# One ring for the first loads, dilated rows of 12 tokens, earlier casts, and spreads moved into their own batch's stage

## The chip, the cores and the metric

The kernel runs on one core of a Trainium2 chip. The time is the device time of one execution in microseconds (us); a smaller one is better. A run of one core has no second die to be compared with, so "fast" below only says that a run lay within 1.5% of the fastest of its kernel. The rule cuts through a scatter without a gap: a run of 356.14 us counts as fast and one of 356.18 as slow, both with a granted clock of 0.986 (the granted clock is the recorded share of TensorE's full clock).

## The reference

Eight batches of eight heads attend over 576 tokens of 64 numbers. The attention output, 4608 tokens of 512 numbers, goes through a two-layer network with a gated activation. Condensed:

```python
rel = pos[:, None] - pos[None, :]
mask_plain = (rel >= 0) & (rel < 32)                             # heads 0 to 3
mask_dil = (rel >= 0) & (rel < 32 * 4) & (rel % 4 == 0)          # heads 4 to 7, every 4th token
attn = softmax(where(mask, q @ k.T / 8, -1e9)) @ v               # (8, 8, 576, 64)
x = attn.transpose(0, 2, 1, 3).reshape(4608, 512)
h = x @ w_in                                                     # 512 x 2048
g = h * (1 / (1 + exp(-beta * h)))
out = g @ w_out                                                  # 2048 x 512
```

Inputs and output are float32; the kernel multiplies in bfloat16.

## The kernel before

The 4608 tokens are worked off in nine blocks of 512. A block is a row of "slots" of four matmuls, 512 columns wide, of about 0.86 us each: 16 h slots (first layer) and, part of them carried into the next block, 16 output slots (second layer). Between the slots lie the small steps of the attention of the next batch: K and Q transpose loaded tokens, S makes scores, V multiplies with v, X transposes the result into `xT`, where the first layer reads it. So TensorE always has something large to do, as long as no step makes it wait.

```python
STEPS = (
    "S20 S21 S22 S23 V20 S30 V21 S31 V22 S32 V23 S33 V30 X20 S00 V31 S01 X21 V32 "
    "S02 V33 S10 V00 X30 S11 V01 S12 X31 V10 X00 V11 X01 X10 X11"
).split()
THIRD = (
    "d0 d1 v3 S20 S21 k0 S22 k1 S23 q0 V20 q1 S30 q2 V21 q3 S31 V22 S32 V23 S33 V30 X20 S00 V31 "
    "S01 X21 V32 S02 V33 v2 S10 V00 X30 S11 V01 S12 X31 V10 X00 V11 X01 X10 X11"
).split()
# FIRST and SECOND (batches 0 and 1) cut
```

The first two batches are loaded as tokens and transposed by TensorE. The rest goes a longer way (a "ring" is the queue into which an engine puts its DMA transfers): GpSimd's ring casts q and k to bfloat16 in DRAM, SyncE's ring loads them transposed, and VectorE then "spreads" them, that is, copies them into tiles in which the other head's half is zero. These copies are the small steps d, k and q.

```python
def load_tok(b, n, x):                      # x = 1: dilated heads
    R, T = (72, 8) if x else (64, 9)        # 72 rows of 8 tokens
    src = {"q": q, "k": k}[n][b, 4 * x:4 * x + 4].rearrange("h (a T) d -> a h (T d)", T=T)
    for lo, hi in ((0, 64), (64, R)):
        if lo < hi:
            nc.gpsimd.dma_start(out=dst[lo:hi], in_=src[lo:hi])

def spread_q(b, n, eng):                    # four of these per batch; k and dilated: two each
    e, hf = n % 2, (n % 2) ^ (n // 2)
    copy_on(eng)(
        out=qq[b % 2][64 * hf:64 * hf + 64, :, :, e],
        in_=raw[b, "q"][64 * e:64 * e + 64].rearrange("p (h i u) -> p h i u", h=4, i=NI))

# extras(b): what is issued beside the steps of batch b, for batch b + 1
    for name, (fn, i) in zip(
            ("S00 S01 S02 V33 S10 S11 S12 V10" if b > 2 else
             "V33 S10 V00 X30 S11 V01 S12 X31").split(), SPREADS):
        at(name, fn, b + 1, i, V)           # all eight spreads, in the second half of the stage
    at("X00", cast_v, b + 1, 3, G)          # v casts on GpSimd, at the stage's end
    at("X01", cast_v, b + 1, 2, G)
```

The order in which the loads enter the rings:

```python
load_vd(0, SQ)                              # v: SyncE's ring
load_vp_1(0, SQ, 0, 1, WIN)
for n in "kq":
    load_tok(0, n, 1)                       # k, q: GpSimd's ring
# ... plain heads of k and q, rest of v, four quarters of w_in
# ... after the steps of batch 0:
for g in range(2): load_w_out(g)
# ... tokens and v of batch 1
for g in range(2, 4): load_w_out(g)
for n in range(4): load_vp(2, G, n * NI, NI)
for kind in "kq": cast_qk(2, kind)
```

The softmax here doesn't subtract the row's maximum and nothing guards it: scores larger than these inputs give would overflow.

## Time and profile before

| | before |
|---|---|
| median of the first three runs | 353.56 us (353.46 to 356.23) |
| span of the profiled run | 352.4 us |
| TensorE busy | 317.4 us, 90% |
| VectorE busy | 209.1 us, 59% |
| longest stage with attention | third batch, 43.5 us; a steady one takes 34.3 |

The table is to be read in this way: the 35 us in which TensorE does nothing are the most that can be won while its own work stays the same, and the last row tells where a large part of them lies. The prediction below shows the lines themselves. To compare kernels I cut each trace where the first h slot of a token block begins, and count the length of each block and the idle time of TensorE in it. In this kernel the first block ends at 67.2 us, the second (with the third batch) at 110.8, the third at 144.4; the next three take 34.3 each, the one after 33.5.

### The profile page before, as it was taken

The numbers are of one execution on the slowest core, as the hardware profiler recorded it, in microseconds if no ns is written. First come the engines' busy times: TensorE is split into PE (matmuls) and PEld (weight loads), VectorE is DVE, ScalarE is ACT, GpSimd is POOL, SyncE is SP. The second block draws the span as 40 slices with busy tenths as digits, with TensorE's granted clock in tenths as the row PEclk, the third lists the DMA queues.
The fourth block names the chain that finished last, engine by engine and source line by source line (L and its number), as shares of the span: only waits on it lengthen the run. The fifth ranks groups of instructions, "written<-read, shape, count | busy, mean of one in ns | idle before, by whom it ended". The sixth has DMA issues, their size and how long they took to land.

```text
span 352.4 us, 6237 instructions
## 1 busy us (share of the span) xinstructions
PE 317.4 (90%) x2357; PEld 169.2 (48%) x2357; DVE 209.1 (59%) x430; ACT 196.2 (56%) x371; POOL 136.8 (39%) x178
## 2 busy tenths in 40 slices
PE   0998989986868998899999999999999999999995
PEld 0774555533433554455545545554555544444442
DVE  4368764679893689357936793688456344334400
ACT  1566756654634675566556656665666555345511
POOL 8954549044472546334643463436433100000000
PEclk9999999999998999999999999999999999999999
DMA  8999999998957990899189919991111111011131
GB/s 165 196 204 201 215 212 159 158 219 131 171 95 156 176 172 30 164 201 166 29 162 159 196 50 178 201 151 33 30 32 32 31 30 59 32 31 32 30 81 67
DMA packets 62671, 42.61 MB, mean 121 GB/s; under 512 B 46145, under 2 KB 56657, under 8 KB 62257
## 3 DMA queue, kind: packets, MB, share of 16 engines
q1 hardware_dynamic: 54128, 24.81, 38.1%
q0 software_dynamic: 8512, 17.40, 27.6%
q8 instruction: 18, 0.29, 0.4%
q14 instruction: 13, 0.10, 0.1%
HBM read 39.32 MB, written 16.52 MB: 158 GB/s over the span
## 4 chain that ended last, share of the span: by engine, by line
PE 79%; DVE 13%; ACT 4%; DMA 2%; issue 1%; POOL 0%; DVEq 0%; ACTq 0%; POOLq 0%
PE h_ps L464 30%; PE o_ps L495 29%; PE h_ps L495 4%; PE at L414 3%; DVE qq L279 3%; PE at L464 3%; PE at L431 3%; DVE xs L421 3%; DVE g L472 2%; PE at L388 2%; DMA xT<-in_k_dram 2%; DVE kz L271 2%; PE at L369 2%; PE at L381 1%; ACT osb L500 1%
## 5 line engine op out<-in xcount | busy, mean ns | idle before, releaser
L472 DVE SCALAR_TENSOR_TENSOR g<-tnh,h_ps 128x512 bf16<-128x512 bf16 x132 | 90.2, 685 | 90.7 <-ACT tnh L469 90.0
L464 PE MATMUL h_ps<-xT,w_in_bf 128*128 128x512 bf16 x528 | 132.9, 379 | 5.0 <-DVE g L472 4.5
L495 PE MATMUL o_ps<-w_out_bf,g 128*128 128x512 bf16 x512 | 130.4, 382 | 3.3 <-ACT osb L500 3.2
L469 ACT ACTIVATE tnh<-h_ps,beta_half 128x512 bf16<-128x512 f32 x132 | 90.7, 687 | 61.8 <-PE h_ps L464 56.3
L464 PEld LDWEIGHTS <-w_in_bf 128*128 128x128 bf16 x576 | 52.9, 98 | 57.4 <-issue 7.1
L495 PEld LDWEIGHTS <-g 128*128 128x128 bf16 x576 | 52.5, 98 | 54.4 <-issue 5.8
L394 ACT ACTIVATE pt<-at 128x384 bf16<-128x384 f32 (+2 forms) x112 | 48.4, 440 | 18.6 <-PE at L388 7.2
L396 POOL TENSOR_TENSOR pt<-pt,mask_d 96x384 bf16<-96x384 bf16 (+1 forms) x48 | 35.6, 752 | 57.4 <-ACT pt L394 56.9
L421 DVE TENSOR_TENSOR xs<-at,rcp 96x256 bf16<-96x256 f32 (+2 forms) x96 | 44.5, 464 | 14.8 <-PE at L431 10.8
L396 POOL TENSOR_TENSOR pt<-pt,mask_PP 128x384 bf16<-128x384 bf16 x24 | 23.6, 985 | 36.4 <-ACT pt L394 36.3
L500 ACT ACTIVATE osb<-o_ps 128x512 f32<-128x512 f32 x32 | 19.1, 597 | 25.6 <-PE o_ps L495 25.5
L414 PEld LDWEIGHTS <-pt 128*128 128x128 bf16 (+2 forms) x448 | 25.7, 101 | 15.0 <-POOL pt L396 2.3
L431 PE MATMUL at<-ident_b,xs 96*128 96x96 bf16 (+1 forms) x224 | 19.4, 203 | 7.2 <-DVE xs L421 4.4
L279 DVE COPY qq<-qpT 64x1152 bf16<-64x1152 bf16 x24 | 21.9, 912 | 0.5
L388 PEld LDWEIGHTS <-kdT 128*96 128x96 bf16 (+1 forms) x128 | 15.4, 128 | 13.9 <-issue 4.0
L388 PE MATMUL at<-qzd,kdT 128*96 128x192 bf16 (+1 forms) x128 | 19.2, 238 | 3.0 <-ACT qzd L357 1.6
L431 PEld LDWEIGHTS <-xs 96*128 96x128 bf16 (+1 forms) x224 | 13.4, 98 | 17.9 <-DVE xs L421 10.0
L414 PE MATMUL at<-vd,pt 96*128 96x65 bf16 (+1 forms) x256 | 19.5, 200 | 0.2 <-POOL pt L396 0.2
L417 DVE RECIPROCAL rcp<-at 96x4 f32<-96x4 f32 (+2 forms) x96 | 16.7, 174 | 3.7 <-PE at L414 3.3
L396 POOL TENSOR_TENSOR pt<-pt,mask_FP 128x384 bf16<-128x384 bf16 x12 | 12.8, 1065 | 15.5 <-ACT pt L394 15.5
L441 ACT COPY xT<-at 128x288 bf16<-128x288 bf16 x24 | 9.4, 398 | 16.5 <-PE at L431 16.5
L495 PE MATMUL h_ps<-w_out_bf,g 128*128 128x512 bf16 x64 | 15.5, 379 | 0.0
(92 smaller groups left out, 232.5 us busy)
## 6 DMA issues: line engine op xcount, KB each, us to landing
vp_st<-in_v_dram SPq DMA_DIRECT2D x10, 384.0 KB, 8.7
qk<-in_k_dram POOLq DMA_DIRECT2D x6, 576.0 KB, 5.5
qk<-in_q_dram POOLq DMA_DIRECT2D x6, 576.0 KB, 8.3
vd_st<-in_v_dram SPq DMA_DIRECT2D x6, 384.0 KB, 5.4
w_in_bf<-in_moe_w_in_dram POOLq DMA_DIRECT2D x4, 512.0 KB, 9.1
w_out_bf<-in_moe_w_out_dram POOLq DMA_DIRECT2D x4, 512.0 KB, 12.8
out_dram<-osb SPq DMA_DIRECT2D x8, 256.0 KB, 3.6
vd_st<-in_v_dram SPq DMA_DIRECT2D x6, 320.0 KB, 6.3
```

The lines of the kernel that those rows point to most:

```text
L279: copy_on(eng)(out=qq[b % 2][64 * hf:64 * hf + 64, :, :, e], in_=raw[b, "q"][64 * e:64 * e + 64].rearrange("p (h i u) -> p h i u", h=4, i=NI))
L388: nc.tensor.matmul(sc[0:K, a, 0:2 * n], lhsT=kd[b][:, rp, h4, DO[hf]:DO[hf] + K], rhs=qzd[b % 2][:, :, rp, h4, hf * DQ[0]:hf * DQ[0] + n], ...
L394: nc.scalar.activation(out=w, in_=sc[0:K, :, 0:2 * n], func=ACT.Exp, scale=SCALE)
L396: nc.gpsimd.tensor_tensor(out=w, in0=w, in1=mask[0:K], op=ALU.mult)
L414: nc.tensor.matmul(pv[:, a, h2, :], lhsT=pt[x][0:K, c:c + P], rhs=rhs, start=True, stop=True)
L421: nc.vector.tensor_tensor(out=xs_t[b, x, jx][:, a0:a0 + m], in0=pv[0:n, :, :, 0:D], in1=rcp[0:n, 0:m].unsqueeze(3).to_broadcast([n, m, 2, ...
L431: nc.tensor.transpose(xp[:, a * n:(a + 1) * n], xs[:, a].rearrange("p h d -> p (h d)"), ident_b[0:n, 0:n])
L464: nc.tensor.matmul(hps, lhsT=w_in_bf[:, kt, fb * P:(fb + 1) * P], rhs=xT[:, kt, t * NTOK:(t + 1) * NTOK], start=(kt == 0), stop=(kt == NKT ...
L469: nc.scalar.activation(out=tnh[:], in_=hps, func=ACT.Tanh, scale=beta_half[:, fb:fb + 1])
L472: nc.vector.scalar_tensor_tensor(out=g[:], in0=tnh[:], scalar=1.0, in1=hps, op0=ALU.add, op1=ALU.mult)
L495: nc.tensor.matmul(ops[:], lhsT=g_t[t, fb][:, tb * P:(tb + 1) * P], rhs=w_out_bf[:, fb, :], start=(fb == 0), stop=(fb == NFB - 1))
L500: nc.scalar.mul(out=osb[:], in_=ops[:], mul=0.5)
```

## The change: its intent, and the diff

VectorE is to lose work where it holds TensorE up. The key and query spreads go from the previous batch's stage to their own batch's, the zero fills to GpSimd, and the third batch's v casts to ScalarE. The start is to come sooner: dilated k and q go first on GpSimd's ring, v behind them, each in one transfer of 48 rows of 12 tokens. And the third batch's casts go ahead of the second half of the output weights, so that its data is there when its stage begins. All of the third batch's v goes to SyncE's ring, and two half groups of h matmuls (H0, H1) go ahead of the first batch's last transposes.

```diff
 STEPS = (
-    "S20 S21 S22 S23 V20 S30 V21 S31 V22 S32 V23 S33 V30 X20 S00 V31 S01 X21 V32 "
+    "S20 S21 S22 k0 S23 k1 V20 S30 q0 V21 S31 q1 V22 S32 q2 V23 S33 q3 V30 X20 S00 V31 S01 X21 V32 "
...                                         (FIRST, SECOND, THIRD in the same way; H0, H1 in FIRST)
-    FROM = {1: 6}
+    FROM = {1: 2}
-        nc.vector.memset(kz[i][64:128, :, :, 0], 0.0)
-        nc.vector.memset(kz[i][0:64, :, :, 1], 0.0)
+            nc.gpsimd.memset(kz[i][64:128, :, :, 0], 0.0)
+            nc.gpsimd.memset(kz[i][0:64, :, :, 1], 0.0)
...                                         (smaller bias tiles, keys of the first batches moved into xT)
-        R, T = (72, 8) if x else (64, 9)
+        R, T = (48, 12) if x else (64, 9)
-        for lo, hi in ((0, 64), (64, R)):
-            if lo < hi:
-                nc.gpsimd.dma_start(out=dst[lo:hi], in_=src[lo:hi])
+        nc.gpsimd.dma_start(out=dst, in_=src)
...                                         (3 instead of 2 transposes per head and pair; crossed query copies)
-            eng = (nc.scalar if b == 1 and name == "v2" else
+            eng = (nc.scalar if name[0] == "v" and (b, name) in ((1, "v2"), (2, "v0"), (2, "v1"), (2, "v2")) else
...                                         (an h group can begin with two of its four matmuls: H0, H1)
-                for name, (fn, i) in zip(
-                        ("S00 S01 S02 V33 S10 S11 S12 V10" if b > 2 else
-                         "V33 S10 V00 X30 S11 V01 S12 X31").split(), SPREADS):
-                    at(name, fn, b + 1, i, V)
+                at("S11", spread_dil, b + 1, 0, V)
+                at("V01", spread_dil, b + 1, 1, V)
-    load_vd(0, SQ)
-    load_vp_1(0, SQ, 0, 1, WIN)
     SQ.dma_start(out=beta_row[:], in_=moe_beta.rearrange("(f p) -> f p", p=P))
     for n in "kq":
         load_tok(0, n, 1)
     make_identity(nc, ident_b[:])
+    load_vd(0, G)
...                                         (another deal of the steps to the slots of the first blocks; a v cast counts as one unit of work)
+    for kind in "kq":
+        cast_qk(2, kind)
     zeros(1)
+    for kind in "kq":
+        load_dil(2, kind)
+    for kind in "kq":
+        load_plain(2, kind)
     for g in range(2, 4):
         load_w_out(g)
-    for n in range(4):
-        load_vp(2, G, n * NI, NI)
-    for kind in "kq":
-        cast_qk(2, kind)
+    zeros_kz()
```

## The prediction

> **What bounds the kernel now.** I read four views. First the page, for the share of each engine; then busy time by stage; then the timeline of TensorE, adding up the idle time in brackets; then the chain of waits, to see what the idle time was spent on.
>
> The page, with its slices of 1/40 of the span (8.8 us each):
>
> ```profile
> PE 317.4 (90%) x2357; PEld 169.2 (48%) x2357; DVE 209.1 (59%) x430; ACT 196.2 (56%) x371; POOL 136.8 (39%) x178
> PE   0998989986868998899999999999999999999995
> DVE  4368764679893689357936793688456344334400
> PEclk9999999999998999999999999999999999999999
> DMA  8999999998957990899189919991111111011131
> ```
>
> TensorE is the bound, with 35 us in which it does nothing, and these 35 us are nearly all in the first 14 slices. Cut by stage (start of batch 0; its rest; the 16 h slots of the first token block; its output slots with the second batch; the block with the third batch; with the fourth; one in steady state):
>
> ```profile
> 0.00:8.70 8.70, 0.01 (x1) 0.04 (x2) 4.30 (x17) 1.49 (x2) 7.22 (x18) 1.00 0.87 165
> 8.70:28.90 20.20, 18.55 (x230) 15.20 (x231) 11.46 (x31) 12.42 (x27) 14.51 (x23) 1.00 1.17 200
> 28.90:43.20 14.30, 14.03 (x68) 6.32 (x69) 11.66 (x22) 10.68 (x16) 7.77 (x11) 1.00 1.15 211
> 43.20:67.20 24.00, 21.33 (x279) 13.91 (x278) 14.62 (x36) 15.05 (x33) 11.84 (x23) 1.00 1.07 181
> 67.20:110.70 43.50, 33.12 (x237) 16.86 (x236) 34.38 (x61) 20.89 (x42) 19.19 (x21) 0.97 0.91 156
> 110.70:144.50 33.80, 30.78 (x238) 16.30 (x237) 24.36 (x48) 20.47 (x41) 16.21 (x18) 0.99 0.71 131
> 178.90:213.20 34.30, 33.47 (x253) 17.76 (x252) 22.91 (x48) 21.53 (x42) 16.63 (x18) 1.00 0.87 145
> ```
>
> Columns: the stretch, its length, busy us of TensorE, weight loads, VectorE, ScalarE, GpSimd; granted clock, DMA share, GB/s. The losses are 8.7 us before the first transpose, 2.7 in 43 to 67, 10.4 in the third batch's stage (67.2 to 110.7), where VectorE is busy 34.4 of 43.5 us, 3.0 in the next, 0.83 in each later one. The last 71 us have no attention, and the change cannot touch them.
>
> Who delays TensorE in the third batch's stage (the chain of waits, in order of time):
>
> ```profile
> 78.51 1.22 DVE kz L271
> 79.75 0.81 DVE kz L271
> 83.38 0.70 DVE kz L139
> 84.27 0.70 DVE kz L140
> 95.63 1.42 DVE vp L310
> ...
> 100.03 1.05 DVE qq L279
> 101.10 1.08 DVE qq L279
> 103.02 1.22 DVE qq L279
> 104.25 1.62 DVE qq L279
> 107.76 3.20 PE o_ps L495 x8
> ```
>
> From 74 to 107 us the chain is almost one line of VectorE work. After the stall TensorE's eight matmuls take 3.20 us instead of 1.73: it restarts at a lower clock, which the eight and the four behind them pay with 1.7 us.
>
> **What the Trainium skill says.** "GPSIMD Engine Reference", section "8. Key points": GpSimd shares its SBUF interfaces with VectorE, with contention when VectorE is in a two-port mode or has two SBUF inputs. The trace agrees: the same query spread (64x1152 bf16) took 0.45 us when GpSimd was idle (81.2 us) and 1.05 to 1.6 us beside its masks and casts (100 to 106 us). "TensorE: Matmul & The Clock Gate", Part 1: an idle array falls back to half its clock. The trace shows it at 107.76 as above. "PSUM — Partial Sum Buffer", section "PSUM bank collisions raise a hardware error": engines on one bank must be kept apart. Here ScalarE's copy of a query tile waits for VectorE's copy of the other half (2.2 us over two waits for qzd, 3.6 over two for qq). "DMA: Bandwidth & Descriptors", section "Issuing engines are not separate DMA queues": all rings run on the same 16 engines and interleave. In the trace 704 KB of v, issued on SyncE at 0.82, landed at 5.1 and 6.6 us; k and q, issued on GpSimd from 1.34, at 8.6 and 9.5.
>
> **The change part by part.**
>
> Start. Dilated k and q now come first on GpSimd's ring, one transfer each instead of two, with v behind them; SyncE's ring has only beta. 288 KB at the 200 KB/us of this stretch take 1.4 us; with issue (1.34 to about 2.1), and about 2 us of start and landing, k should be there at about 5.5 and q at 6.8 instead of 8.55 and 9.5. Against it: rows of 12 tokens make three transposes per head and pair instead of two, 48 instead of 32; one took 2.08/32 = 65 ns, so +1.0 us here. K from 5.5 to 7.1, Q to 8.7. Then the query copies: the two tiles go in crossed order, so VectorE (0.71) and ScalarE (0.65) work on different banks; the tile of the first score block is ready after about 1.4 us, at 10.1, instead of 11.8. The smaller bias tiles (96 and 48 columns instead of 384 and 192) save GpSimd about 2.5 us of building, so the next loads are issued earlier. Gain **2.0 us** (estimate, 1.3 to 2.6). From there to 28.9 TensorE has no gap over 0.2 us until 27.6, so the shift carries through.
>
> End of batch 0. Half of two h groups (dilated heads) goes ahead of the last transposes: four matmuls, 0.86 us, into gaps of 0.46, 0.46 and 0.27. **-0.7**.
>
> First block, with the second batch. Its steps now start at the 11th slot, one per slot, and no longer all after the h slots. Gone are the waits for qzd (1.42 + 0.17) and for qq (0.74): the transposes have one to three slots of 0.86 us to be copied behind. Of 2.7 us I take off 2.2; 16 more transposes at 1.20/32 = 37 ns add 0.6. **-1.6**.
>
> Third batch's stage. Its casts go ahead of half the output weights, and 768 KB of its v leave GpSimd's ring for a later place on SyncE's. The casts landed at 57.0 and 60.9, the last transposing load at 71.7, and the stage's steps began at 75. Moved up, I estimate casts at 46 to 49 and the last load at about 60. VectorE loses here: the key and query spreads of the fourth batch, 0.55 + 0.56 + 2.14 + 2.86 = 6.1 us; two zero fills, 1.4 (the other two lie just before the stage; all go to GpSimd, early); the v casts, 1.22 + 1.42 = 2.6, now on ScalarE at about 3 us. That is 10.1 of 34.4. What is left, 24 us, must fit into TensorE's time. That floor: the steady stage has 32 slots of 0.865 = 27.7 us, 0.83 idle, so its attention costs 34.3 - 27.7 - 0.8 = 5.8; this stage has 28 slots, 24.2 + 5.8 = 30.0. ScalarE would have 24, VectorE 24 of it, so it is tight, and I give it 0.8 of the ordinary idle time and 2 of new stalls: 32.8 instead of 43.5, **-10.7**.
>
> Fourth batch's stage. TensorE's gaps of 0.74 and 1.34 behind VectorE's spreads go (they are now early in the stage), with about 0.3 of slow clock at its start. **-2.4**.
>
> Later stages. The same eight spreads per stage, moved from the second half to the first, where four divisions and GpSimd's masks also are. I add **+0.5** over five stages for new waits.
>
> Output weights. Their third quarter landed at 47.2 and was used at 57.9; behind 1152 KB of casts and beside the transposing loads I estimate it lands at 51 to 54 and is wanted at 53. **+0.4**.
>
> Sum: -2.0 - 0.7 - 1.6 - 10.7 - 2.4 + 0.5 + 0.4 = -16.5; 353.6 - 16.5 = **337 us**.
>
> **The rivals.**
> (1) ScalarE takes VectorE's place. It gets 3 us of casts into a stage that shrinks by 11, and a cast waiting for v would hold up every tanh behind it. For it: ScalarE serves tanh, exp and copies strictly in order, and v of the third batch is now issued behind four transposing loads. Against: 24 of 33 us, and 4 us of estimated slack for v. It would give back 3 to 5 us: 341.
> (2) The DMA rings set the time. The 16 engines are full until 53 us in both kernels, and the order alone changes. If the output weights come 3 us late or the transposing loads at 65, TensorE waits in 50 to 65: 341 to 343. Against: neither was waited for before, by 10 us for the weights.
> (3) The start does not move: the first load's time is latency and not sharing. Then 339.
> (4) The crowded first half of the later stages costs 1 us each: 341. For it: spreads are doubled in length by GpSimd; against, VectorE is busy only 23 of 34 us there.
> (5) The stage reaches its floor, and the start gains more: 333.
>
> **Range and chances.** The large term, VectorE's 10 us on the chain, is well supported; what can fail is what replaces it. One or two of the rivals together give 341 to 343, the good case 332. The 2% line is 346.5, so two thirds of the gain must fail to miss it. **Range 332 to 343**; faster by over 2% 0.93, within 2% 0.06, slower 0.01.
>
> **What would show it.** The first transpose at about 5.5 us (8.7 before) and the first bias matmul of scores with its keys at about 10; the first output slots' gaps behind qzd and qq gone; in the third batch's stage TensorE idle under 3.5 us, VectorE about 24 us busy, no slow matmuls at its end; its length near 33 us; the later stages near 34.3. It would be wrong if TensorE showed waits on ScalarE's tanh behind v casts, on output weights around 53 us, or on VectorE's g behind spreads in each later stage.

## The result, and the profile after

The changed kernel took 342.57 us (median of four runs, 341.58 to 343.61) where the kernel before took 354.76 on the same chip (four runs). The ratio is 0.9655, with a 95% interval from 0.9598 to 0.9713. Here and below a ratio is the mean time of one kernel's fast runs over that of the other's of the same rounds, so it is not quite the ratio of the quoted medians. The result is correct.

The page of the changed kernel; of the slices, each is 8.5 us long:

```profile
PE 311.3 (92%) x2347; PEld 168.0 (49%) x2389; DVE 194.0 (57%) x424; ACT 197.8 (58%) x374; POOL 129.7 (38%) x170
PE   1899996997899899999999999999999999999994
DVE  4578773469657774767386637763865344244400
DMA  6999999999899794979698968882001210011121
GB/s 109 211 207 208 166 233 176 198 217 205 141 141 189 128 197 102 172 182 129 131 142 183 127 125 160 176 124 63 18 14 33 62 33 32 32 31 33 41 82 62
```

VectorE is busy 15 us less, and TensorE's 86868 in the 9th to 13th slice (its line in the prediction) has become 97897. Two new things show. In the first slice the DMA engines move 109 GB/s, where it was 165. And TensorE has a 6 in its 7th slice, 51 to 59 us, where it had a 9.

What sets the end has changed hands. This is the head of the chain of waits on both pages, the kernel before first:

```profile
PE 79%; DVE 13%; ACT 4%; DMA 2%; issue 1%; POOL 0%; DVEq 0%; ACTq 0%; POOLq 0%
```

```profile
PE 72%; DMA 13%; DVE 4%; ACT 4%; POOL 3%; issue 2%; POOLq 0%; ACTq 0%
```

VectorE's 13% have become 4%, as intended; DMA's 2% have become 13%. A chain follows one path only, so 13% is no loss of 13%; but it says which kind of wait to look for.

By stage (until the first transpose; rest of batch 0; first token block; third batch's stage; the fourth's; one in steady state; columns as in the prediction; here and below some stretches begin or end 0.1 to 0.3 us before the first h slot):

```profile
0.00:6.50 6.50, 0.00 (x0) 0.00 (x0) 2.78 (x15) 1.49 (x2) 5.05 (x16) 1.00 0.58 89
6.50:24.90 18.40, 16.19 (x228) 13.56 (x229) 11.00 (x29) 10.48 (x24) 13.31 (x22) 1.00 1.17 205
24.90:66.40 41.50, 36.96 (x375) 21.34 (x380) 27.32 (x61) 26.35 (x52) 20.65 (x31) 1.00 1.18 198
66.40:101.50 35.10, 30.50 (x234) 16.16 (x238) 23.58 (x50) 24.04 (x46) 15.60 (x18) 1.00 0.96 176
101.50:133.20 31.70, 29.81 (x234) 16.10 (x237) 22.17 (x48) 20.55 (x41) 16.18 (x19) 1.00 0.86 155
166.80:200.40 33.60, 32.94 (x248) 17.76 (x252) 21.47 (x48) 21.44 (x42) 16.09 (x18) 1.00 0.89 151
```

VectorE's busy time in the third batch's stage (fourth line) fell from 34.4 to 23.6 us, and TensorE's idle time there from 10.4 to 4.6. The first block begins at about 25 partly because half an h group now goes ahead (without it, in a run below, it begins at 26.0, against 29.0 in the kernel before); it is its end that can be compared. The stages by the starts of their first h slots, with what each was predicted to give:

| stage | before | after | difference | predicted |
|---|---|---|---|---|
| end of the first block | 67.2 | 66.4 | -0.8 | -3.9 (start, half groups, first block, weights) |
| third batch's stage | 43.5 | 35.2 | -8.3 | -10.7 |
| fourth batch's stage | 33.7 | 31.7 | -2.0 | -2.4 |
| the next four | 34.3, 34.3, 34.3, 33.5 | 33.6 each | -2.0 | +0.5 |
| the last two, without attention | 28.5, 43.1 | 28.5, 43.5 | +0.4 | 0 |
| whole span | 352.4 | 339.9 | -12.5 | -16.5 |

(The parts are rounded.) Most of what is missing against the prediction lies ahead of 67 us. TensorE's timeline of the kernel before at its first work (start, length, what; in brackets the idle time before it and its releaser):

```profile
8.69 2.08 PE L328 MATMUL at<-ident_b,xT 72*128 72x72 bf16 x32 [8.69 <-DMA xT<-in_k_dram]
...
11.79 0.48 PE L388 MATMUL at<-qzd,kdT 128*96 128x192 bf16 x2 [0.69 <-DVE qzd L357]
```

The changed kernel, at its first work and at 54 us:

```profile
6.54 1.14 PE L327 MATMUL at<-ident_b,xT 48*128 48x48 bf16 x24 [6.54 <-POOL neg_d L162]
8.63 1.14 PE L327 MATMUL at<-ident_b,xT 48*128 48x48 bf16 x24 [0.96 <-DMA xT<-in_q_dram]
...
11.04 0.48 PE L391 MATMUL at<-qzd,kdT 128*96 128x192 bf16 x2 [0.78 <-ACT qzd L357]
...
53.93 0.33 PE L378 MATMUL at<-qq,xT 128*128 128x192 bf16 x2
57.38 1.02 PE L508 MATMUL h_ps<-w_out_bf,g 128*128 128x512 bf16 x4 [3.12 <-DMA w_out_bf<-in_moe_w_out_dram]
```

The first transpose starts 2.15 us sooner (the first bracket names GpSimd, but the keys landed at 6.49, so it is the load that counts). Then the new wait: q lands at 8.59, and TensorE stands for 0.96 us between the keys' transposes and the queries'. The first scores with keys gain only 0.75 us. And at 57.38 an output slot had waited 3.12 us for the third quarter of the output weights. It landed at 57.3; before it landed at 47.2.

A second thing differs in this stretch. The same pair of score matmuls at about the same time, in the kernel before and in the changed one:

```profile
22.49 0.53 PE L375 MATMUL at<-qq,kz 128*128 128x192 bf16 x2
```

```profile
22.19 0.33 PE L378 MATMUL at<-qq,xT 128*128 128x192 bf16 x2
```

In both traces these small matmuls are slow at first, one taking up to 0.37 us, and 0.24 us later. The trace's first record of the full clock stands at 25.9 us in the kernel before and at 21.9 in the changed one; the clock column of the stretches above shows 1.00 there all the same, because it counts only recorded lowered stretches. This time is not a fixed property of a kernel: in the traces of the experiments it lies anywhere from 14.6 to 27.9 us.

The third batch's stage is no longer a line of VectorE work. The chain of waits there (start, us, what) now reads:

```profile
75.70 1.03 ACT vd L312
...
78.07 1.03 DVE kz L270
...
80.36 0.76 DVE qq L278
...
82.91 0.47 DVE qq L278
...
84.81 0.46 DVE qq L278
85.27 0.47 DVE qq L278
85.78 0.33 PE at L384 x4
...
100.16 1.67 PE o_ps L508 x7
```

The query spreads are the third batch's own; the fourth's, which took 1.05 to 1.62 us each at the end of this stage before, are gone from it. So is the slow clock: seven matmuls at 100.16 take 1.67 us.

The later stages got shorter, which I had not expected. The end of one of them, kernel before, TensorE and then VectorE:

```profile
210.41 0.30 PE L431 MATMUL at<-ident_b,xs 96*128 96x96 bf16 x3
211.18 0.30 PE L431 MATMUL at<-ident_b,xs 96*128 96x96 bf16 x3 [0.46 <-ACT xT L441]
```

```profile
206.74 0.80 DVE L279 COPY qq<-qpT 64x1152 bf16<-64x1152 bf16 x1
208.29 1.31 DVE L279 COPY qq<-qpT 64x1152 bf16<-64x1152 bf16 x1
210.56 0.55 DVE L421 TENSOR_TENSOR xs<-at,rcp 96x384 bf16<-96x384 f32 x1
```

And in the changed kernel:

```profile
198.64 0.42 PE L434 MATMUL at<-ident_b,xs 96*128 96x96 bf16 x6
198.90 1.89 PE L508 MATMUL o_ps<-w_out_bf,g 128*128 128x512 bf16 x8
```

Before, the next batch's last spreads ran beside GpSimd's v casts just when the last normalisations (`xs`) were due. The last two groups of transposes came one after the other, with 0.46 us of idle time between them, and the stage ended on that. Now the six transposes go in one group. In the prediction I had looked at where the spreads were going and not at what they had held up where they were.

### The profile page after: what moved, and what is told of

It is laid out like the page before. It is cut to its first block, busy times and chain, and to the rows that moved or that the text cites. A ratio compares the mean times of both kernels' runs of the same rounds, so it can differ in the third digit from the quotient of the medians.

```text
span 339.9 us, 6236 instructions
## 1 busy us (share of the span) xinstructions
PE 311.3 (92%) x2347; PEld 168.0 (49%) x2389; DVE 194.0 (57%) x424; ACT 197.8 (58%) x374; POOL 129.7 (38%) x170
## 4 chain that ended last, share of the span: by engine, by line
PE 72%; DMA 13%; DVE 4%; ACT 4%; POOL 3%; issue 2%; POOLq 0%; ACTq 0%
PE o_ps L508 31%; PE h_ps L475 29%; DMA w_out_bf<-in_moe_w_out_dram 5%; DMA xT<-in_q_dram 5%; PE h_ps L508 3%; DMA vp_st<-in_v_dram 3%; PE at L417 3%; PE at L434 2%; PE at L384 2%; ACT osb L513 2%; DVE g L485 2%; PE at L391 2%; DVE qq L278 1%; ACT tnh L482 1%; POOL pt L399 1%
## 5 line engine op out<-in xcount | busy, mean ns | idle before, releaser
L485 DVE SCALAR_TENSOR_TENSOR g<-tnh,h_ps 128x512 bf16<-128x512 bf16 x130 | 88.7, 684 | 90.4 <-ACT tnh L482 89.6
L475 PE MATMUL h_ps<-xT,w_in_bf 128*128 128x512 bf16 x504 | 129.6, 379 | 3.3 <-DVE g L485 2.1
L508 PE MATMUL o_ps<-w_out_bf,g 128*128 128x512 bf16 x494 | 126.3, 379 | 4.7 <-ACT osb L513 3.8
L482 ACT ACTIVATE tnh<-h_ps,beta_half 128x512 bf16<-128x512 f32 x130 | 89.3, 687 | 56.3 <-PE h_ps L475 51.9
L475 PEld LDWEIGHTS <-w_in_bf 128*128 128x128 bf16 x576 | 51.7, 98 | 51.5 <-issue 3.5
L399 POOL TENSOR_TENSOR pt<-pt,mask_d 96x384 bf16<-96x384 bf16 (+1 forms) x48 | 36.9, 778 | 52.0 <-ACT pt L397 51.4
L399 POOL TENSOR_TENSOR pt<-pt,mask_PP 128x384 bf16<-128x384 bf16 x24 | 22.8, 949 | 37.8 <-ACT pt L397 37.7
L434 PE MATMUL at<-ident_b,xs 96*128 96x96 bf16 (+1 forms) x224 | 18.1, 200 | 1.1 <-DVE xs L424 1.0
L399 POOL TENSOR_TENSOR pt<-pt,mask_FP 128x384 bf16<-128x384 bf16 x12 | 10.9, 910 | 16.0 <-ACT pt L397 16.0
L448 ACT COPY xT<-at 128x384 bf16<-128x384 bf16 (+1 forms) x32 | 12.6, 394 | 3.5 <-PE at L434 3.5
```

Of the source, the lines that this page charges most:

```text
L399: nc.gpsimd.tensor_tensor(out=w, in0=w, in1=mask[0:K], op=ALU.mult)
L434: nc.tensor.transpose(xp[:, a * n:(a + 1) * n], xs[:, a].rearrange("p h d -> p (h d)"), ident_b[0:n, 0:n])
L475: nc.tensor.matmul(hps, lhsT=w_in_bf[:, kt, fb * P:(fb + 1) * P], rhs=xT[:, kt, t * NTOK:(t + 1) * NTOK], start=(kt == 2), stop=(kt == 1))
L482: nc.scalar.activation(out=tnh[:], in_=hps, func=ACT.Tanh, scale=beta_half[:, fb:fb + 1])
L485: nc.vector.scalar_tensor_tensor(out=g[:], in0=tnh[:], scalar=1.0, in1=hps, op0=ALU.add, op1=ALU.mult)
L508: nc.tensor.matmul(ops[:], lhsT=g_t[t, fb][:, tb * P:(tb + 1) * P], rhs=w_out_bf[:, fb, :], start=(fb == 0), stop=(fb == NFB - 1))
```

## The experiments

Each run is compared with runs of the kernel before on the same chip. The changed kernel itself ran beside them only in the last call; where a difference to the change is given in us for the earlier runs, it is one of medians from different calls, and the ratios to the kernel before show it smaller or not at all (their intervals often overlap with that of the change). In the call with four of the runs (the kernel before with the spreads moved, v casts on VectorE, rows of 8, no early half) three of the seven runs of the kernel before were slow; the record calls these four comparisons unclear at its 2% line. What carries the readings are the traces: the length of a stage that an edit does not touch repeats within 0.1 us from trace to trace. Theory A is that the change is worth what it takes off VectorE's chain, above all by the spreads, and that the rest of the expected gain was lost in the order and the speed of GpSimd's DMA ring. The rivals are named with each run.

### The casts behind the weights again

```diff
+    for g in range(2, 4):
+        load_w_out(g)
     for kind in "kq":
         cast_qk(2, kind)
...
-    for g in range(2, 4):
-        load_w_out(g)
```

> The changed kernel with one part undone: the second half of the output weights goes ahead of the third batch's casts again. The theory that the order on GpSimd's ring is what TensorE's 3.12 us wait at 57.4 us pays for: the third quarter of the weights lands about 4 to 5 us earlier (near 52) and that wait is gone, while the casts and the transposing loads land about 5 us later (last near 69) and the third batch's first steps wait for them: 1 to 4 us come back at about 68 us. Net 340 to 345 us. Rival, that the early casts are worth most of the third stage's gain: over 347 us, with VectorE and TensorE idle for over 4 us at the third batch's start. Rival, that the third stage has slack for late casts: 339 to 340, the wait simply gone.

Measured: 339.20 us (338.75 to 339.49), ratio to before 0.9612 [0.9560, 0.9664]. The first block and the third batch's stage of this kernel:

```profile
25.40:64.00 38.60, 37.31 (x381) 21.27 (x378) 27.83 (x61) 26.28 (x52) 18.64 (x27) 1.00 1.13 190
64.00:99.10 35.10, 30.76 (x239) 16.15 (x238) 23.58 (x50) 24.13 (x46) 17.02 (x21) 1.00 1.07 198
```

The expected 340 to 345 us was too high; the last rival, slack in the third stage, is what came. The first block is idle 1.3 us instead of 4.5, the wait for the weights is gone, and yet the third batch's stage takes the same time as in the change, though its casts landed at 56.5 and 59.2 instead of 51.3 and 54.1 and its last transposing load at 66.7 instead of 64.3. So the earlier casts gained nothing, and cost about 3 us (2.4 between the two traces, 3.4 between the medians). That last load had been at 71.7 in the kernel before, with casts at 57.0 and 60.9: with the transposing loads issued right behind the casts it lands 7.5 us after the last cast instead of 10.8. Whether the stage needs even that was not tried.

### v on SyncE's ring again

```diff
+    load_vd(0, SQ)
+    load_vp_1(0, SQ, 0, 1, WIN)
     SQ.dma_start(out=beta_row[:], ...)
...
-    load_vd(0, G)
...
-    load_vp_1(0, G, 0, 1, WIN)
```

> The changed kernel with the first v loads back on SyncE's ring at the start. Theory that one ring alone starts slowly and shifts all that stands behind it: the first transposes start later, at 8 us instead of 6.5, but the last input weights land about 1.5 to 2 us earlier (26.5 to 27 instead of 28.6) and the wait for the output weights shrinks from 3.1 to 1.3 to 2 us; total within 1 us of the changed kernel (341.5 to 343.5). Rival, that the ring makes no difference to the total of what the engines move: input weights land at the same time, the start's loss of 1.5 us stays in full, 343.5 to 344.5.

Measured: 341.33 us (340.56 to 342.90), ratio 0.9679 [0.9627, 0.9730]. The first stretch and the first block:

```profile
0.00:9.20 9.20, 0.01 (x1) 0.01 (x1) 2.78 (x15) 1.49 (x2) 7.45 (x22) 1.00 0.95 153
28.70:66.70 38.00, 37.02 (x382) 21.19 (x380) 27.25 (x61) 26.27 (x52) 18.94 (x29) 1.00 1.19 196
```

The first transpose starts at 9.19, 2.65 us later than in the changed kernel. But the DMA engines are busy from the start (153 GB/s over the first 9.2 us; 89 over the first 6.5 in the changed kernel), the last input weights land at 27.9 instead of 28.6, the first block has no wait for output weights (idle 0.98), and it ends at 66.7 instead of 66.4. The 2.65 us that the new order gains at the start are paid back at 54 us by the ring.

### The k and q spreads back in the previous batch's stage

```diff
-    "S20 S21 S22 k0 S23 k1 V20 S30 q0 V21 S31 q1 V22 S32 q2 V23 S33 q3 V30 ..."
+    "S20 S21 S22 S23 V20 S30 V21 S31 V22 S32 V23 S33 V30 ..."
...
+                for name, (fn, i) in zip(
+                        ("S02 V33 S10 V00 S12 V10" if b > 2 else
+                         "V00 X30 S11 V01 S12 X31").split(),
+                        [(spread_k, 0), (spread_k, 1)] + [(spread_q, n) for n in range(4)]):
+                    at(name, fn, b + 1, i, V)
```

> The changed kernel with the key and query spreads of the fourth and later batches back in the stage before their own, in its second half. Theory that they cost VectorE time on the chain at the end of each stage: the third batch's stage grows by 3 to 5 us, and each later stage by 0.5 to 0.7 (last transposes wait again, a gap near 0.46 us before the last one): 346 to 350 us. Rival, that the gain of the later stages came from somewhere else (the order of the h groups' halves, PSUM banks): later stages stay at 33.6 and only the third grows.

Measured: 357.64 us (357.33 to 358.17), ratio 1.0137 [1.0091, 1.0182], so 15 us slower than the change. That is beyond the expected 346 to 350. The third batch's stage, the fourth's and a later one:

```profile
68.10:108.30 40.20, 32.59 (x238) 16.52 (x238) 28.89 (x56) 24.18 (x46) 16.84 (x18) 0.96 0.92 169
108.30:144.40 36.10, 31.42 (x238) 16.41 (x237) 25.11 (x48) 20.47 (x41) 16.32 (x18) 0.97 0.71 130
215.00:249.90 34.90, 33.48 (x253) 17.75 (x252) 22.64 (x48) 21.53 (x42) 15.17 (x16) 1.00 0.75 134
```

And TensorE at the end of that later stage:

```profile
247.51 0.30 PE L434 MATMUL at<-ident_b,xs 96*128 96x96 bf16 x3
248.27 0.30 PE L434 MATMUL at<-ident_b,xs 96*128 96x96 bf16 x3 [0.46 <-ACT xT L444]
```

VectorE's 5.3 us come back into the third batch's stage and cost 5.2 us there (from first h slot to first h slot); the fourth's pays 4.4, the next three 1.3 to 1.9 each, and the 0.46 us gap before the last transposes is back. Some of it is clock: three stretches at half clock, 3.4 us each, lie in this run, at 57, 105 and 143 us. The places that I chose for the spreads are a little worse than those of the kernel before (34.9 us against 34.3 in a later stage), so 15 us is more than the move of the change itself is worth.

### The kernel before with the spreads moved, and nothing else of the change

```diff
-    "S20 S21 S22 S23 V20 S30 V21 S31 V22 S32 V23 S33 V30 ..."
+    "S20 S21 S22 k0 S23 k1 V20 S30 q0 V21 S31 q1 V22 S32 q2 V23 S33 q3 V30 ..."
...
-                for name, (fn, i) in zip((...), SPREADS):
-                    at(name, fn, b + 1, i, V)
+                at("S11", spread_dil, b + 1, 0, V)
+                at("V01", spread_dil, b + 1, 1, V)
...                                         (the transposing loads of the later batches, some steps later)
```

> The kernel before with one part of the change alone: the key and query spreads of the fourth and later batches move into their own batch's stage (first half), with the loads of the plain heads one step group later. Putting them back cost the changed kernel 15 us. If they are the main part, the kernel before gains 7 to 12 us here: the third batch's stage falls from 43.3 to 36 to 39 us and each steady stage from 34.3 to 33.6; total 342 to 347. Rival, that the 15 us were the fault of the places chosen when they were put back: a gain of 2 to 5 us only, with the third batch's stage over 40.

Measured: 344.30 us (342.17 to 346.55), ratio 0.9744 [0.9625, 0.9863], that is some 9 us of the change's 12 (5 to 13 by the interval). The profiled run was the slowest of the four. The same three stages:

```profile
68.40:106.90 38.50, 31.59 (x238) 16.52 (x237) 28.01 (x55) 21.01 (x43) 17.34 (x19) 1.00 0.74 135
106.90:138.60 31.70, 30.04 (x238) 16.09 (x237) 22.16 (x48) 20.57 (x41) 16.46 (x20) 1.00 0.89 154
205.80:239.40 33.60, 33.21 (x253) 17.79 (x252) 21.45 (x48) 21.46 (x42) 15.11 (x16) 1.00 0.74 139
```

The fourth batch's stage and the later ones have exactly the lengths of the changed kernel, 31.7 and 33.6. So all of the gain there is the spreads'. The third batch's stage went from 43.5 to 38.4 with this part alone; the other 3.2 us come from the rest. By stage the part gives 5.1 + 2.0 + 2.0, which is the same 9 us.

Where the 3.2 us lie can be seen, though not which edit takes them away. In this run TensorE still waits 1.70 us at 88.15 for VectorE's `g`, soon after two zero fills (84.78 and 85.68, 0.70 us each), and 1.32 us at 98.60 for the cast of the plain heads' v, 1.62 us long. In the changed kernel its waits in this stage are 1.08 us at most, and the second of these two is gone even with that cast back on VectorE (next run). That leaves the zero fills and the new order of the steps as candidates.

### The third batch's v casts on VectorE

```diff
-            eng = (nc.scalar if name[0] == "v" and (b, name) in ((1, "v2"), (2, "v0"), (2, "v1"), (2, "v2")) else
+            eng = (nc.scalar if name[0] == "v" and (b, name) in ((1, "v2"),) else
```

> The changed kernel with the third batch's v casts on VectorE instead of ScalarE. If VectorE is still the engine that TensorE waits for in the third batch's stage (gaps of 1.08 and 0.75 us behind it), 2.9 us more on it lengthen that stage from 35.1 to 36.5 to 38 us: total 344 to 345.5. Rival, that ScalarE with its 3.5 us of casts has become the bound there: the stage gets shorter, under 34.5.

Measured: 344.38 us (343.64 to 344.42), ratio 0.9740 [0.9649, 0.9832]. A stretch of the first block and the third batch's stage:

```profile
56.20:63.00 6.80, 5.75 (x27) 2.65 (x27) 0.32 (x2) 0.91 (x3) 0.00 (x0) 0.50 1.29 182
68.90:104.30 35.40, 30.90 (x238) 16.21 (x239) 25.47 (x53) 21.19 (x43) 16.24 (x18) 1.00 0.84 159
```

The stage takes 0.3 us longer than in the change, with VectorE at 25.5 and ScalarE at 21.2 us. It matters little which of the two does the casts; neither "ScalarE becomes the bound" nor "VectorE is so near its limit that they had to go" holds. What makes this profiled run longer is the first line: 2.2 us into a wait of 3.29 us for the output weights the granted clock fell to 0.50 for 6.8 us, and the first block took 44.1 us. That belongs to the wait, not to the casts. So the total lies within the expected 344 to 345.5 by luck: the stage was to grow to 36.5 or more, and did not.

### Rows of 8 tokens again

```diff
-        R, T = (48, 12) if x else (64, 9)
+        R, T = (72, 8) if x else (64, 9)
...
-        nc.gpsimd.dma_start(out=dst, in_=src)
+        for lo, hi in ((0, 64), (64, R)):
+            if lo < hi:
+                nc.gpsimd.dma_start(out=dst[lo:hi], in_=src[lo:hi])
```

> The changed kernel with rows of 8 tokens instead of 12 for the dilated heads (two transfers per load again, 32 instead of 48 transposes per batch). The second batch's dilated k and q took 2.2 and 2.7 us of the full ring with rows of 12, and 1.1 and 1.3 with rows of 8 in the kernel before. Theory that rows of 12 cost the ring about 2.5 us and TensorE 1.5: the third quarter of the output weights lands 2 to 3 us earlier, the wait of 3.1 us shrinks below 1, total 338.5 to 340.5. Rival, that the tokens' loads were slow for another reason (their place in memory, the load of other engines at 34 to 40 us): they stay at over 2 us each, and the total stays within 1 us of the changed kernel.

Measured: 338.36 us (337.77 to 339.23), ratio 0.9577 [0.9485, 0.9669]. The wait for the weights, and the first block:

```profile
53.58 1.02 PE L510 MATMUL h_ps<-w_out_bf,g 128*128 128x512 bf16 x4 [0.55 <-DMA w_out_bf<-in_moe_w_out_dram]
```

```profile
24.40:62.60 38.20, 36.40 (x366) 21.07 (x364) 27.16 (x61) 26.27 (x52) 21.56 (x32) 1.00 1.15 205
```

With the change's own order of casts and weights the wait is 0.55 us instead of 3.12: the third quarter of the weights landed at 53.5, nearly 4 us sooner. Both forms carry the same 288 KB for each of k and q. On the full ring of the second batch the loads of 48 rows each came 2.2 and 2.7 us behind the load before them, the loads of 72 rows 1.0 and 1.3 us behind (in the kernel before; in this run itself q comes 1.35 us behind k, against 2.7 in the change). So it is the shape of the loads that was slow. Which property of it (3 KB instead of 2 KB pieces, 48 rows instead of 64 and 8) the runs do not tell.

### Half of the output weights not loaded

The second half of the weights is never loaded and the first half used twice. The result is wrong; the shapes are kept.

```diff
-    for g in range(2, 4):
-        load_w_out(g)
...
-                ops[:], lhsT=..., rhs=w_out_bf[:, fb, :],
+                ops[:], lhsT=..., rhs=w_out_bf[:, fb % 8, :],
```

> Wrong result on purpose: the second half of the output weights is never loaded, the first half is used twice. It takes away the wait for those weights and 1 MB of loads and nothing else. Theory: the 3.1 us wait is gone, the transposing loads land about 3 us earlier, and the total falls by 3 to 4 us to 338 to 339.5. Rival, that the wait only hides the next one (the third batch's loads, ScalarE, VectorE): the time falls by less than 1.5 us, and idle time of the same size appears in the third batch's stage.

Measured: 338.56 us (337.80 to 341.49), ratio 0.9610 [0.9546, 0.9674]; about 4 us less than the change. That is roughly what the wait for the weights, with its clock, is worth, and two correct kernels reach it by other means. The profiled run was the slowest: it waited 1.98 us for the second batch's keys at 37 us, and the clock was halved for 6.8 us from 38.6 on.

### No early half of an h group

```diff
-    "... V10 H0 X00 V11 H1 X01 X10 X11"
+    "... V10 X00 V11 X01 X10 X11"
```

> The changed kernel without the two half groups of h ahead of the last transposes of the first batch. The gaps of 0.46 and 0.27 us at 27 to 28 us become 0.46, 0.46 and 0.27 and 0.86 us of matmuls come after them: the first block's h slots end about 0.7 us later. But the wait for the output weights at 57.4 us, set by the ring, takes that up: total within 0.7 us of the changed kernel, the wait 0.7 us shorter. Rival, that it costs its 0.7 us or more in full: 343.2 to 343.8.

Measured: 342.00 us (340.92 to 343.73), ratio 0.9694 [0.9564, 0.9825]; the wait for the weights is 3.12 us as in the change. No effect can be told; in this trace the full clock was first granted at 14.6 us, which hides a difference of 0.7 us.

### Combinations, and the change once more

Four kernels with five rounds each on one chip, where the kernel before took 353.90 us (median of eleven runs, two of them slow): rows of 8 with the weights first; that with v on SyncE's ring; that with work units given to the k and q steps, so that they spread over more slots; and the change itself.

```diff
 (rows of 8 and weights first: the two edits shown above)
 (v on SyncE's ring: the edit shown above, in addition)
-    WORK = {..., "k": 0, "q": 0, "v": 1}
+    WORK = {..., "k": 1, "q": 1, "v": 1}
```

> The changed kernel with two parts undone that each gained alone: rows of 8 tokens, and the weights ahead of the casts. If both gains are the same 3.1 us wait for the output weights, they do not add: with rows of 8 the wait was down to 0.55 us, so the order adds that and no more, 337.3 to 338.3 us. If the late casts now bind the third batch (TensorE arrives there 4 us earlier than in the changed kernel) it gets slower than rows of 8 alone: over 339.

> The one before with the first v loads back on SyncE's ring. In the changed kernel this cost 2.65 us at the first transposes and nothing in the total, as the wait for the weights took it up. Where no such wait is left, the later start must show: 2 to 2.6 us more than the kernel without it, 339.5 to 340.5. Rival: the rings' better use at the start repays it again: within 0.7 us.

> As the first of these, with the spreads counted as one unit of work each where the steps are dealt out to the slots, so that they lie further apart. If the gaps of 1.08, 0.75 and 1.28 us behind VectorE in the third and fourth batch's stages come from spreads that follow each other too closely, they shrink: 335.5 to 337. If from VectorE's sum of work, no change (within 0.7 us).

> The changed kernel itself, as the control of the same call: 341.5 to 343.6 us. Its spread comes from the wait of 3.1 us for the weights: where it trips TensorE's clock to a half for 3.4 or 6.8 us the run is 1.7 to 3.4 us longer; the kernels without the wait should agree within 0.5 us or so.

| kernel | median | ratio to before, 95% |
|---|---|---|
| rows of 8, weights first | 338.71 | 0.9566 [0.9519, 0.9612] |
| with v on SyncE's ring | 338.97 | 0.9583 [0.9547, 0.9620] |
| with work units for spreads | 337.89 | 0.9556 [0.9515, 0.9596] |
| the change again | 343.49 | 0.9719 [0.9684, 0.9754] |

The two gains, rows of 8 and weights first, do not add: alone they gave 338.4 and 339.2, together 338.7. Either takes away the same wait. The three combinations cannot be told apart, and are about 1.5% faster than the change, here on the same chip (4.8 us between the medians of the first and the last row). The work units shorten the fourth batch's stage from 31.7 to 31.1 us and lengthen each later one by 0.1; the expected 335.5 to 337 was not reached. The starts with v on GpSimd's ring and on SyncE's:

```profile
5.90 1.12 PE L329 MATMUL at<-ident_b,xT 72*128 72x72 bf16 x16 [5.90 <-DMA xT<-in_k_dram]
8.71 1.12 PE L329 MATMUL at<-ident_b,xT 72*128 72x72 bf16 x16 [1.69 <-DMA xT<-in_q_dram]
...
11.09 0.48 PE L393 MATMUL at<-qzd,kdT 128*96 128x192 bf16 x2 [0.92 <-ACT qzd L359]
```

```profile
8.32 2.30 PE L329 MATMUL at<-ident_b,xT 72*128 72x72 bf16 x32 [8.32 <-DMA xT<-in_k_dram]
...
11.88 0.47 PE L393 MATMUL at<-qzd,kdT 128*96 128x192 bf16 x2 [0.92 <-ACT qzd L359]
```

The first transpose is 2.4 us sooner on one ring, the first scores only 0.8, because the second load, q, comes 2.8 us behind the first. The first block ends at 63.9 with one ring and at 63.5 with two. So the placement of v is neutral here too, now with no wait for the weights that could hide a gain; the expected loss of 2 to 2.6 us did not come.

The control also shows the clock. In its profiled run the wait for the weights was 2.81 us, and then:

```profile
57.90:61.30 3.40, 3.18 (x17) 1.77 (x17) 0.17 (x1) 0.49 (x1) 0.00 (x0) 0.50 1.36 157
```

Half the clock for 3.4 us; each such stretch costs about 1.7 us (estimate: half of 3.4). In the first profiled run of the change it did not happen after 3.12 us of waiting (granted clock 0.999, span 339.9); the other three runs there had 0.994 and spans of 340.9 to 341.9. But the wait is not the only source of scatter. The kernels without it were expected to agree within 0.5 us and did not: six runs of the first combination, with granted clocks of 0.995 to 1.0, took 336.14 to 339.94 us. The varying time of the first full clock, which these numbers leave out, may be part of it; that is not shown.

## Why the prediction was right or wrong

The direction and the range held: 342.57 us measured, 337 predicted, 332 to 343 given, and the 2% line passed with more than 3%. The range held by 0.4 us only; the control run later measured 343.49, just outside it. The main mechanism is shown from both sides: moving the spreads alone gave about three quarters of the gain on the kernel before, and putting the k and q spreads back took all of it from the changed kernel. The centre was 5.6 us too low. In the two traces the span fell by 12.5 where the sum said 16.5; that is 4.0 of it, and the rest is that the profiled run of the change was its fastest and that of the kernel before was 0.6 us above its median. Where the 4.0 come from, step by step:

- **Start, -2.0.** The keys were put at 5.5 us and came at 6.49, the queries at 6.8 and 8.59. The failed term is the time of the two transfers: 1.4 us each at the stretch's 200 KB/us, where the DMA engines moved 89 over these 6.5 us and q came 2.1 us behind k. Rival 3 came half true: the keys, with v out of the way, came 2.1 us sooner (6.49 instead of 8.55), not 3. The transposes were over-sized: 48 of them took 2.28 us (twice 1.14), 0.2 more than 32 had, not 1.0. First scores with keys: -0.75. And yet the eighth h slot is done 2.5 us sooner (tanh at 33.96 instead of 36.49), close to the 2.7 that start and half groups were to give together. That is in part luck: the full clock came at 21.9 instead of 25.9, that is 10.9 us after the first scores instead of 14.1, and 3.2 us less at half speed are worth up to 1.6 us (estimate). The part that the order of the rings brings does not carry through to the end, as the two runs with v on SyncE's ring show: what the ring does not move in the first 9 us it moves later.
- **Half groups, -0.7.** Not to be seen: without them the time was 342.0 with an interval that reaches to both sides.
- **First block, -1.6.** Not separable by the total of the change, but the versions in which the wait for the weights is short or gone, and the first loads are on one ring, end it at 62.6 to 64.0 instead of 67.2. So start, half groups and first block together give 3.2 to 4.6 us there, a part of it clock, where 4.3 were predicted: the sum was about right, and the wait took it back.
- **Output weights, +0.4.** This is the step that failed most. "I estimate it lands at 51 to 54 and is wanted at 53": it was wanted at 54.3 and landed at 57.3. The sum can be made from the traces: 47.2 before, plus 1152 KB of casts at 200 KB/us, 5.8; plus 1.4 because the quarter ahead of it landed at 34.3 and not 32.9 (the slow start); plus 2.6 because the second batch's dilated k and q took 2.2 + 2.7 us and not 1.0 + 1.3. That is 57.0. (Read from the landings: the load ahead of the casts landed 3.8 us later, the casts took 5.3, the quarter itself 3.3 instead of 2.1.) The prediction had only the first term. And the slot wanted it 3.7 us sooner than before (54.3 instead of 57.9). Rival 2 had the event and its size, weights 3 us late and 341 to 343, and I gave it too little weight, on the ground that they had had 10 us to spare: the change itself spent them.
- **Third batch's stage, -10.7.** It gave -8.3. VectorE came out at 23.6 us against 24 predicted and no slow clock was left; the term that was too small is the idle time, 2.8 us assumed and 4.6 measured (4.3 in traces in which no matmul record is missing), in pieces of 0.2 to 1.1 us, several of them behind VectorE. The floor was too low as well: 30.0 us of TensorE work assumed, 30.6 to 30.9 measured. Rival 1 falls: ScalarE was busy 24.0 us as counted, but the casts on VectorE gave the same stage. Of the parts, the spreads gave -5.1. The v casts' engine gave 0.3 at most and the early casts nothing. The other 3.2 us lie among the zero fills, the transposing loads issued earlier and the new order of steps; I did not split them, so that stays open.
- **Fourth batch's stage, -2.4.** It gave -2.0, and the spreads alone give all of it.
- **Later stages, +0.5.** Wrong in sign: -2.0 over four stages. Rival 4 falls. The failed step is that I asked only what the spreads would meet in the first half. At their old place they were doubled in length by GpSimd's v casts (0.80 and 1.31 us, against 0.46 alone in the third batch's stage) and delayed the last normalisations. At their new place one of four takes 0.60 us, beside the mask of the dilated heads, and the others 0.46. This error, 2.5 us, covered part of the others; that the sum came no lower than it did is luck to that extent.
- **Two slips of the working.** The 35 idle us are not "nearly all" in the first 14 slices: all stages up to the fourth batch's lose 26.7 of them. And the gain that must fail to miss the 2% line is 9.4 of 16.5, less than two thirds.

Of the parts of the change, one carries it, two cost 4 to 5 us together by the same wait, and undoing either gives most of that back (rows of 12, casts ahead of weights), and three are neutral within what could be measured (one ring for the first loads, half groups, v casts' engine). The zero fills on GpSimd, the crossed query copies and the smaller bias tiles were not tried alone.

## What to carry to other kernels

When an operation is moved off a chain, read its old place as closely as its new one: what ran beside it there and what was due right behind it. When something is put ahead of something else on a full ring, add up everything that changed ahead of the late item, and not only the item itself; a spare time of 10 us is a budget that three small changes can spend. And undo the parts one by one afterwards: here two parts that were to bring data sooner cost 4 to 5 us together, and the kernel without them is about 1.5% faster.

## What the Trainium skill lacked or had wrong

- "DMA: Bandwidth & Descriptors", section "Rules for kernel authors", advises against two transfers to disjoint partition halves and for a single one of 128 partitions. Here one transfer of 48 rows instead of two of 64 and 8 rows made the kernel slower, 342.6 against 338.4 us: 2.2 and 2.7 us on a full ring against 1.0 and 1.3 for the same 288 KB. Rows, length of the pieces and number of transfers changed together and no load had 128 rows, so this does not test the advice. The page gives no times of loads by their number of rows at equal size.
- "TensorE: Matmul & The Clock Gate", Part 1, ties the fall to half the clock to an idle window of about 3.4 us that runs freely. The stretches here agree, 3.4 or 6.8 us long. But the waits before or around them were shorter than that, 1.98, 2.81, 3.15 and 3.29 us, and in the kernel before with the spreads moved the clock was halved from 29.2 us on with two waits of 0.46 us ahead of it, while two waits of 3.12 us were followed by none. Part 1 gives no chance for such shorter waits.
- "GPSIMD Engine Reference", section "8. Key points", names the contention with VectorE without a size. A 64x1152 bfloat16 copy on VectorE took 0.45 to 0.46 us with GpSimd idle, 0.60 beside GpSimd's mask of the dilated heads (changed kernel, later stages), and 0.80 to 2.10 beside its plain masks and v casts (kernel before).
